# A squeeze-and-excite gate on one core: larger resident slots, reads and stores cut into pieces at the turn between its two passes

## The chip, the cores and the metric

The kernel runs on one core of a Trainium2 chip. The metric is device time in microseconds (us). Every time below is the median of fast runs. Executions of one kernel agree within about 0.2%, so differences of half a microsecond can be told apart when the kernels ran on the same chip in turn. "Span" is the length of the one execution that was profiled; it is about 1.9 us shorter than the timed run.

In the profile, PE is the matmul engine (TensorE) and PEld its weight loads, DVE is VectorE, ACT is ScalarE, POOL is GpSimd and SP is SyncE; a q after the name is that engine's DMA queue. SBUF is the on-chip memory for data, PSUM the one that matmuls write to. "DMA share" is the mean busy share of the core's 16 DMA engines (in short stretches it can read a little over 1), and PEclk is the granted clock of PE as a share of full speed.

## The reference

```python
# x: (1, 256, 256, 384) bf16; w_down: (384, 24); w_up: (24, 384)
def reference(x, w_down, w_up):
    s = x.mean(axis=(1, 2))
    s = _sigmoid(_silu(s @ w_down) @ w_up)
    return x * s[:, None, None, :]
```

The gate needs the mean over the whole input before the first output element can be made. The input is 50.33 MB and does not fit into SBUF. So the kernel makes two passes: it reads everything once for the mean, keeps what it can, and reads the rest a second time.

## The kernel before

Each partition holds 512 rows of 384 bf16 elements; one row over 128 partitions is 128 x 768 = 98,304 B. The rows are cut into 32 chunks of 16. There are 16 slots of one chunk each. In the read phase, PE sums every row with a matmul against ones. The last 16 chunks stay resident. In the second phase VectorE multiplies a chunk in its slot, the ACT queue stores it, and the SP queue reads a missing chunk into a slot whose store has landed.

```python
            def _(sp):                                       # SP queue
                sp.dma_start(wd_sb[:, :, :], ...).then_inc(sem_w, 16)      # weights first
                sp.dma_start(wu_sb[0:RED, :], w_up[:, :]).then_inc(sem_w, 16)
                for t in range(NCH):                         # read phase: 32 chunks of 16 rows
                    ...
                    if t >= S:
                        sp.wait_ge(sem_pe, t - S + 1)
                    sp.dma_start(slots[s][:, 0:nr, :], xr[:, rs:rs + nr, :]).then_inc(sem_rd[s], 16)
                for i, (c, s, is_stream) in enumerate(items):  # second reads
                    ...
                    sp.wait_ge(sem_wr[s], 16 * item_wr_before[i])
                    sp.dma_start(slots[s][:, 0:nr, :], ...).then_inc(sem_rd[s], 16)
            ...
            def _(act):
                ...
                act.wait_ge(sem_pe, NCH)
                for k in range(NK):                          # mean: three copies out of PSUM
                    act.activation(mean3[32 * k:32 * k + 1, 0:P], ps_S[0:1, k * P:(k + 1) * P], ACTF.Copy, scale=inv_count).then_inc(sem_mean3, 1)
                ...
                for i, (c, s, is_stream) in enumerate(items):
                    act.wait_ge(sem_dve, i + 1)              # VectorE: one multiply per chunk
                    act.dma_start(outr[:, rs:rs + nr, :], slots[s][:, 0:nr, :]).then_inc(sem_wr[s], 16)
```

## Time and profile before

| Reading (before) | Value |
|---|---|
| time | 314.41 us (span 312.5) |
| HBM read / written | 75.53 MB / 50.33 MB |
| rate, read phase / second phase | 425 / 430 GB/s |
| first read issued | 1.75 us |
| last read's matmuls start | 123.82 us |
| first multiply starts | 129.64 us |
| first store issued | 133.03 us |

The page of the kernel before, its span in 40 slices (each 7.8 us): busy tenths of each engine, DMA busy tenths and the rate; and the bytes.

```profile
PE   0977787777777777200000000000000000000000
DVE  0000000000000000499999999994444444000000
...
DMA  7999999999999996099999999999999999999998
GB/s 250 431 428 422 425 428 422 425 426 423 425 424 423 425 426 254 0 377 327 429 428 429 429 428 433 433 431 433 429 429 428 429 428 429 429 431 431 433 433 357
...
HBM read 75.53 MB, written 50.33 MB: 403 GB/s over the span
```

The DMA row is full except at the start, the end and one hole at slices 15 and 16 (counted from 0). PE never fills a slice for long and VectorE is idle half of the second phase, so neither sets the pace.

Busy times by stretch, before: start and length in us, busy time (instructions) of each engine, granted PE clock, DMA share, rate.

```profile
core 0: us, PE busy (x) PEld busy (x) DVE busy (x) ACT busy (x) POOL busy (x), PEclk, DMA share, GB/s
8.00:104.00 96.00, 74.36 (x415) 39.22 (x414) 0.00 (x0) 0.00 (x0) 0.00 (x0) 0.98 1.01 425
160.00:260.00 100.00, 0.00 (x0) 0.00 (x0) 72.31 (x23) 0.00 (x0) 0.00 (x0) 0.50 1.01 430
122.00:133.60 11.60, 4.42 (x27) 2.11 (x25) 4.40 (x4) 1.45 (x5) 0.00 (x0) 0.87 0.02 8
```

The first two stretches are at the pace of the DMA engines. In the third, 11.6 us long, the DMA share is 0.02: it stands still. What it waits for is in the timeline of the kernel before (start us, length us, engine, line, instruction, and in brackets the idle time before it).

```profile
0.73 0.42 SPq L136 DMA_DIRECT2D se_wd<-in_w_down_dram  x1
1.21 0.48 SPq L137 DMA_DIRECT2D se_wu<-in_w_up_dram  x1
1.75 11.70 SPq L143 DMA_DIRECT2D se_slot<-in_x_dram  x12
...
123.82 2.77 PE L193 MATMUL se_psS<-se_slot,se_ones 128*32 128x384 bf16 x16 [0.90 <-DMA se_slot<-in_x_dram]
126.63 0.84 ACT L227 ACTIVATE se_mean<-se_psS 1x128 bf16<-1x128 f32 x3 [124.40 <-PE se_psS L193]
...
129.12 0.49 ACT L236 ACTIVATE se_sbc<-se_psu 128x384 bf16<-128x384 f32 x1 [0.74 <-PE se_psu L218]
129.64 6.63 DVE L175 TENSOR_TENSOR se_slot<-se_slot,se_sbc 128x6144 bf16<-128x6144 bf16 x2 [0.95 <-ACT se_sbc L236]
133.03 0.38 ACTq L240 DMA_DIRECT2D out_dram<-se_slot  x1
```

After the last read has landed, PE still has the whole last chunk to sum (2.77 us), ACT copies the mean (0.84), a chain of small steps makes the gate, and VectorE multiplies a whole chunk (3.35 us each) before the first store can be issued.

### The profile page before, as it was taken

The numbers are of one execution on the slowest core, as the hardware profiler recorded it, in microseconds if no ns is written. First come the engines' busy times: TensorE is split into PE (matmuls) and PEld (weight loads), VectorE is DVE, ScalarE is ACT, GpSimd is POOL, SyncE is SP. The second block draws the span as 40 slices with busy tenths as digits, with TensorE's granted clock in tenths as the row PEclk, the third lists the DMA queues.
The fourth block names the chain that finished last, engine by engine and source line by source line (L and its number), as shares of the span: only waits on it lengthen the run. The fifth ranks groups of instructions, "written<-read, shape, count | busy, mean of one in ns | idle before, by whom it ended". The sixth has DMA issues, their size and how long they took to land.

```text
span 312.5 us, 1205 instructions
## 1 busy us (share of the span) xinstructions
PE 92.3 (30%) x517; PEld 48.5 (16%) x517; DVE 106.2 (34%) x40; ACT 2.9 (1%) x7; POOL 0.2 (0%) x4
## 2 busy tenths in 40 slices
PE   0977787777777777200000000000000000000000
PEld 0444344444333444100000000000000000000000
DVE  0000000000000000499999999994444444000000
ACT  1000000000000000100000000000000000000000
POOL 0000000000000000000000000000000000000000
PEclk9999799999999999855555555555555555555555
DMA  7999999999999996099999999999999999999998
GB/s 250 431 428 422 425 428 422 425 426 423 425 424 423 425 426 254 0 377 327 429 428 429 429 428 433 433 431 433 429 429 428 429 428 429 429 431 431 433 433 357
DMA packets 11960, 125.94 MB, mean 403 GB/s; under 512 B 1692, under 2 KB 1716, under 8 KB 1716
## 3 DMA queue, kind: packets, MB, share of 16 engines
q1 hardware_dynamic: 7348, 75.54, 57.7%
q10 hardware_dynamic: 4608, 50.33, 38.1%
q8 instruction: 4, 0.07, 0.1%
HBM read 75.53 MB, written 50.33 MB: 403 GB/s over the span
## 4 chain that ended last, share of the span: by engine, by line
DMA 56%; DVE 14%; another core or an unknown queue 9%; PE 2%; SPq 2%; ACT 0%; issue 0%
DMA se_slot<-in_x_dram 40%; DMA out_dram<-se_slot 16%; DVE se_slot L175 14%; PE se_psS L193 2%; SPq L143 1%; SPq L149 0%; ACT se_mean L227 0%; ACT se_sbc L236 0%; SPq L137 0%; SPq L136 0%; PE se_psu L218 0%; DVE se_dT L165 0%; PE se_psd L209 0%; PE se_psmT L204 0%
## 5 line engine op out<-in xcount | busy, mean ns | idle before, releaser
L175 DVE TENSOR_TENSOR se_slot<-se_slot,se_sbc 128x6144 bf16<-128x6144 bf16 x32 | 105.4, 3353 | 28.6 <-DMA se_slot<-in_x_dram 27.7
L193 PE MATMUL se_psS<-se_slot,se_ones 128*32 128x384 bf16 x512 | 91.5, 334 | 35.1 <-DMA se_slot<-in_x_dram 35.1
L193 PEld LDWEIGHTS se_psS<-se_slot,se_ones 128*32 128x32 bf16 x512 | 48.2, 99 | 78.0 <-DMA se_slot<-in_x_dram 38.4
L162 DVE CAST se_meanT<-se_psmT 128x3 bf16<-128x3 f32 x1 | 0.2, 164 | 126.4 <-PE se_psmT L204 126.4
L227 ACT ACTIVATE se_mean<-se_psS 1x128 bf16<-1x128 f32 x3 | 0.8, 265 | 124.4 <-PE se_psS L193 124.4
L223 ACT ACT_TABLE_LOAD x1 | 1.3, 1283 | 0.7 <-PEq L255 0.7
L218 PE MATMUL se_psu<-se_wu,se_dT 24*128 24x384 bf16 x1 | 0.3, 332 | 0.6 <-DVE se_dT L165 0.6
L236 ACT ACTIVATE se_sbc<-se_psu 128x384 bf16<-128x384 f32 x1 | 0.5, 490 | 0.7 <-PE se_psu L218 0.7
L204 PE MATMUL se_psmT<-se_sel,se_mean 65*128 65x3 bf16 x1 | 0.2, 178 | 0.9 <-ACT se_mean L227 0.9
L165 DVE TENSOR_TENSOR se_dT<-se_psd,se_sig 24x128 bf16<-24x128 f32 x1 | 0.3, 279 | 0.5 <-ACT se_sig L234 0.5
L155 DVE MEMSET se_ones<- 128x32 bf16 x1 | 0.1, 85 | 0.8 <-PEq L255 0.8
L204 PEld LDWEIGHTS se_psmT<-se_sel,se_mean 65*128 65x128 bf16 x1 | 0.1, 96 | 1.3 <-ACT se_mean L227 1.3
L209 PE MATMUL se_psd<-se_meanT,se_wd 128*24 128x1 bf16 x3 | 0.2, 167 | 0.3 <-DVE se_meanT L162 0.3
L160 DVE MEMSET se_sel<- 1x1 bf16 x3 | 0.2, 59 | 0.2
L223 ACT ACTIVATE se_warm<-se_ones 1x8 bf16<-1x8 bf16 x1 | 0.2, 208 | 0.0
L218 PEld LDWEIGHTS se_psu<-se_wu,se_dT 24*128 24x128 bf16 x1 | 0.1, 91 | 0.7 <-DVE se_dT L165 0.7
L209 PEld LDWEIGHTS se_psd<-se_meanT,se_wd 128*24 128x24 bf16 x3 | 0.1, 90 | 0.3 <-DVE se_meanT L162 0.3
L234 ACT ACTIVATE se_sig<-se_psd 24x1 f32<-24x1 f32 x1 | 0.2, 160 | 0.8 <-PE se_psd L209 0.8
L156 DVE MEMSET se_mean<- 128x64 uint32 x1 | 0.1, 112 | 0.0
L255 POOL MEMSET const-bfloat16-1.0<- 128x1 bf16 x1 | 0.1, 101 | 0.0
L255 POOL MEMSET const-uint8-127<- 128x1 uint8 x1 | 0.1, 101 | 0.0
L255 POOL MEMSET const-float32-0.0<- 128x1 f32 x1 | 0.1, 98 | 0.2 <-issue 0.2
(2 smaller groups left out, 0.2 us busy)
## 6 DMA issues: line engine op xcount, KB each, us to landing
se_slot<-in_x_dram SPq DMA_DIRECT2D x48, 1536.0 KB, 31.5
out_dram<-se_slot ACTq DMA_DIRECT2D x32, 1536.0 KB, 43.7
se_wd<-in_w_down_dram SPq DMA_DIRECT2D x1, 18.0 KB
se_wu<-in_w_up_dram SPq DMA_DIRECT2D x1, 18.0 KB
```

The source lines that it names most:

```text
L143: sp.dma_start(slots[s][:, 0:nr, :], xr[:, rs:rs + nr, :]).then_inc(sem_rd[s], 16)
L160: v.memset(sel[32 * k:32 * k + 1, k:k + 1], 1.0).then_inc(sem_init, 1)
L165: v.tensor_tensor(dT[0:RED, 0:P], ps_d[0:RED, 0:1].broadcast_to([RED, P]), sig[0:RED, 0:1].broadcast_to([RED, P]), ALU.mult,).then_inc(sem ...
L175: v.tensor_tensor(slots[s][:, 0:nr, :], slots[s][:, 0:nr, :], s_bc[:, None, :].broadcast_to([P, nr, C]), ALU.mult,).then_inc(sem_dve, 1)
L193: ins = pe.matmul(ps_S[0:M1, 0:C], ones[:, 0:M1], slots[s][:, r, :], start=(mm_i == 0), stop=(mm_i == n_mm - 1),)
L204: pe.matmul(ps_mT[:, 0:NK], mean3[0:32 * (NK - 1) + 1, 0:P], sel[0:32 * (NK - 1) + 1, 0:NK]).then_inc(sem_mT, 1)
L209: ins = pe.matmul(ps_d[0:RED, 0:1], wd_sb[:, k, 0:RED], meanT[:, k:k + 1], start=(k == 0), stop=(k == NK - 1),)
L218: pe.matmul(ps_u[:, 0:C], dT[0:RED, 0:P], wu_sb[0:RED, 0:C]).then_inc(sem_u, 1)
L223: act.activation(warm[0:1, 0:8], ones[0:1, 0:8], ACTF.Sigmoid)
L227: act.activation(mean3[32 * k:32 * k + 1, 0:P], ps_S[0:1, k * P:(k + 1) * P], ACTF.Copy, scale=inv_count,).then_inc(sem_mean3, 1)
L236: act.activation(s_bc[:, 0:C], ps_u[:, 0:C], ACTF.Sigmoid).then_inc(sem_sbc, 1)
L255: nc = _bacc.Bacc("TRN2", target_bir_lowering=False, num_devices=1)
```

## The change

The change keeps the two passes and their order. It makes the slots larger and fewer (14 of 21 rows, 294 rows resident instead of 256, with a smaller reserve for dynamic DMA to make room), cuts the last reads and the first stores into pieces, takes the mean with one VectorE instruction, and moves the weight loads from the head of the SP queue to the ACT queue, late in the read phase. The new GpSimd path and the scratch slot are off with the default arguments.

```diff
-        R = max(1, min(RPP, (16 * 1024) // (C * 2)))
+        R = max(1, min(RPP, 21))                       # chunks: 8 rows, then 24 of 21
...
-        S_fit = max(1, (avail - 1024) // (slot_bytes + 64))
+        S_fit = max(1, (avail - 64) // slot_bytes)     # 14 slots
...
+        piece_plan = _phase1_read_pieces(chunks)
+        # last four chunks: [4,17] [9,12] [6,8,7] [3,5,4,3,2,2,2] rows
...
+            elif s == 0:
+                pieces = make_pieces(nr, list(first_item_pieces))      # 2, 4, 4, 5, 6
+            elif s == 1 or (s == 2 and 1 in pool_slot_set):
+                pieces = make_pieces(nr, [6, 7, 8])
+            elif s == 2:
+                pieces = make_pieces(nr, [10, 11])
+            else:
+                pieces = [(0, nr)]
...
             def _(sp):
-                sp.dma_start(wd_sb[:, :, :], ...)
-                sp.dma_start(wu_sb[0:RED, :], ...)
...
             def _(v):
+                v.wait_ge(sem_pe, NCH)
+                v.tensor_scalar(out=meanr[0:1, 0:C], in0=ps_S[0:1, 0:C], scalar1=inv_count, ...)
...
             def _(act):
-                for k in range(NK):
-                    act.activation(mean3[...], ps_S[...], ACTF.Copy, scale=inv_count)
+                act.wait_ge(sem_pe, max(0, NCH - 3))
+                act.dma_start(wd_sb[:, :, :], ...)
+                act.dma_start(wu_sb[0:RED, :], ...)
...
-    nc = _bacc.Bacc("TRN2", target_bir_lowering=False, num_devices=1)
+    nc = _bacc.Bacc("TRN2", target_bir_lowering=False, num_devices=1, dynamic_dma_scratch_size=256)
```

More of the change, by code (lines that the diff above doesn't have):

```diff
@@ L1, with _phase1_read_pieces @@
 import contextlib
-import math
 import concourse.bass as bass
 from concourse import mybir
+def _phase1_read_pieces(chunks, pe_rate_frac=0.24, min_piece=2, extra=2):
+    pieces_per_chunk = {}
+    rem = 0
+    plan = []
+    for t in reversed(range(len(chunks))):
+        nr = chunks[t][1]
+        cuts_rev = []
+        left = nr
+        while left > 0:
+            cap = max(min_piece, int(pe_rate_frac * rem) + extra)
+            sz = min(left, cap)
+            cuts_rev.append(sz)
+            rem += sz
+            left -= sz
+        sizes = list(reversed(cuts_rev))
+        lo = 0
+        pl = []
+        for sz in sizes:
+            pl.append((lo, lo + sz))
+            lo += sz
+        pieces_per_chunk[t] = pl
+        if len(pl) == 1 and sizes[0] == nr and rem - nr >= 4 * nr:
+            break
+    for t in range(len(chunks)):
+        if t in pieces_per_chunk:
+            plan.append(pieces_per_chunk[t])
+        else:
+            plan.append([(0, chunks[t][1])])
+    return plan
 def bass_standalone__se_block__vision_kernel(
@@ L16, in bass_standalone__se_block__vision_kernel @@
     max_slots=None,
+    use_scratch=False,
+    first_item_pieces=(2, 4, 4, 5, 6),
+    pool_slots=(),
+    pool_piece_rows=7,
 ):
@@ L37, in bass_standalone__se_block__vision_kernel @@
     if rows_per_chunk is None:
-        R = max(1, min(RPP, (16 * 1024) // (C * 2)))
-        while R > 1 and RPP % R != 0:
-            R -= 1
+        R = max(1, min(RPP, 21))
     else:
-        R = int(rows_per_chunk)
+        R = max(1, min(int(rows_per_chunk), RPP))
     chunks = []
+    rem0 = RPP % R
     rs = 0
+    if rem0:
+        chunks.append((0, rem0))
+        rs = rem0
     while rs < RPP:
-        nr = min(R, RPP - rs)
-        chunks.append((rs, nr))
-        rs += nr
+        chunks.append((rs, R))
+        rs += R
     NCH = len(chunks)
@@ L60, in bass_standalone__se_block__vision_kernel @@
         s_bc = E(nc.sbuf_tensor("se_sbc", [P, C], bf16))
-        mean3 = E(nc.sbuf_tensor("se_mean3", [P, P], bf16))
-        sel = E(nc.sbuf_tensor("se_sel", [P, NK], bf16))
+        meanr = E(nc.sbuf_tensor("se_meanr", [P, C], bf16))
         meanT = E(nc.sbuf_tensor("se_meanT", [P, NK], bf16))
@@ L67, in bass_standalone__se_block__vision_kernel @@
         dT = E(nc.sbuf_tensor("se_dT", [P, P], bf16))
-        warm = E(nc.sbuf_tensor("se_warm", [P, 8], bf16))
         ps_S = E(nc.psum_tensor("se_psS", [P, C], f32))
-        ps_mT = E(nc.psum_tensor("se_psmT", [P, NK], f32))
+        ps_mT = E(nc.psum_tensor("se_psmT", [P, NK * 512], f32))
         ps_d = E(nc.psum_tensor("se_psd", [P, 1], f32))
@@ L76, in bass_standalone__se_block__vision_kernel @@
         avail = nc.sbuf_bytes_remaining
-        S_fit = max(1, (avail - 1024) // (slot_bytes + 64))
-        S = min(NCH, S_fit)
+        S_fit = max(1, (avail - 64) // slot_bytes)
+        slots = []
+        if use_scratch and nc.dynamic_dma_scratch_size is not None and nc.dynamic_dma_scratch_size >= slot_bytes:
+            slots.append(nc.alloc_sbuf_tensor_at("se_slot_scr", [P, R, C], bf16, offset=0))
+        S = S_fit + len(slots)
+        S = min(NCH, S)
         if max_slots is not None:
@@ L81, in bass_standalone__se_block__vision_kernel @@
         assert S >= 2 or NCH == 1
-        slots = [E(nc.sbuf_tensor(f"se_slot{i}", [P, R, C], bf16)) for i in range(S)]
+        while len(slots) < S:
+            slots.append(E(nc.sbuf_tensor(f"se_slot{len(slots)}", [P, R, C], bf16)))
+        slots = slots[:S]
         sem_rd = [E(nc.semaphore(f"se_rd{i}")) for i in range(S)]
@@ L89, in bass_standalone__se_block__vision_kernel @@
         sem_ones = E(nc.semaphore("se_onesm"))
-        sem_z = E(nc.semaphore("se_z"))
-        sem_init = E(nc.semaphore("se_init"))
-        sem_mean3 = E(nc.semaphore("se_m3"))
+        sem_mean = E(nc.semaphore("se_mean"))
         sem_mT = E(nc.semaphore("se_mT"))
@@ L99, in bass_standalone__se_block__vision_kernel @@
         sem_sbc = E(nc.semaphore("se_sbcs"))
+        sem_pool = E(nc.semaphore("se_pool"))
         slot_of_chunk = [t % S for t in range(NCH)]
@@ L103, in bass_standalone__se_block__vision_kernel @@
         resident_chunk_of_slot = [max(t for t in range(NCH) if t % S == s) for s in range(S)]
-        items = []
-        for s in range(S):
-            items.append((resident_chunk_of_slot[s], s, False))
-        for b in range(NB):
-            items.append((b, b % S, True))
-        assert len(items) == NCH
-        assert sorted(c for c, _, _ in items) == list(range(NCH))
         fill_cnt = [0] * S
-        wr_cnt = [0] * S
         phase1_fill_idx = []
@@ L118, in bass_standalone__se_block__vision_kernel @@
             phase1_fill_idx.append(fill_cnt[s])
-        item_fill_idx = []
-        item_wr_before = []
-        fill_cnt2 = list(fill_cnt)
-        for (c, s, is_stream) in items:
-            if is_stream:
-                item_wr_before.append(wr_cnt[s])
-                fill_cnt2[s] += 1
-                item_fill_idx.append(fill_cnt2[s])
-            else:
-                item_wr_before.append(None)
-                item_fill_idx.append(phase1_fill_idx[c])
-            wr_cnt[s] += 1
+        piece_plan = _phase1_read_pieces(chunks)
@@ new lines, in bass_standalone__se_block__vision_kernel @@
+        p1_pieces = []
+        extra_piece_sems = 0
+        for t in range(NCH):
+            s = slot_of_chunk[t]
+            pl = []
+            for i, (lo, hi) in enumerate(piece_plan[t]):
+                if i == 0:
+                    pl.append((lo, hi, sem_rd[s], 16 * phase1_fill_idx[t]))
+                else:
+                    sm = E(nc.semaphore(f"se_p1x{extra_piece_sems}"))
+                    extra_piece_sems += 1
+                    pl.append((lo, hi, sm, 16))
+            p1_pieces.append(pl)
@@ new lines, in bass_standalone__se_block__vision_kernel, with make_pieces @@
+        assert extra_piece_sems <= 16
+        def make_pieces(nr, sizes):
+            cuts = [0]
+            for z in sizes:
+                cuts.append(min(nr, cuts[-1] + z))
+            if cuts[-1] < nr:
+                cuts.append(nr)
+            cuts = sorted(set(cuts))
+            return [(cuts[i], cuts[i + 1]) for i in range(len(cuts) - 1)]
+        pool_slot_set = set(int(ps) for ps in pool_slots if 0 <= int(ps) < S)
+        items = []
+        for s in range(S):
+            c = resident_chunk_of_slot[s]
+            nr = chunks[c][1]
+            eng = "pool" if s in pool_slot_set else "dve"
+            if eng == "pool":
+                k = max(1, -(-nr // max(1, int(pool_piece_rows))))
+                base = [nr // k] * k
+                for i in range(nr - sum(base)):
+                    base[i] += 1
+                pieces = make_pieces(nr, base)
+            elif s == 0:
[4 more added lines that the diff above has]
+                pieces = make_pieces(nr, [10, 11])
+            else:
+                pieces = [(0, nr)]
+            items.append(dict(chunk=c, slot=s, stream=False, eng=eng, pieces=pieces, fill_idx=phase1_fill_idx[c]))
@@ new lines, in bass_standalone__se_block__vision_kernel @@
+        wr_cnt = [0] * S
+        fill_cnt2 = list(fill_cnt)
+        for it in items:
+            it["wr_before"] = None
+            wr_cnt[it["slot"]] += len(it["pieces"])
+        for b in range(NB):
+            s = b % S
+            it = dict(chunk=b, slot=s, stream=True, eng="dve", pieces=[(0, chunks[b][1])])
+            it["wr_before"] = wr_cnt[s]
+            fill_cnt2[s] += 1
+            it["fill_idx"] = fill_cnt2[s]
+            wr_cnt[s] += len(it["pieces"])
+            items.append(it)
@@ L131, in bass_standalone__se_block__vision_kernel @@
         total_wr = list(wr_cnt)
+        assert sorted(it["chunk"] for it in items) == list(range(NCH))
         with nc.Block() as block:
@@ L135, in _ @@
             def _(sp):
-                sp.dma_start(wd_sb[:, :, :], w_down.rearrange("(k p) r -> p k r", p=P)).then_inc(sem_w, 16)
-                sp.dma_start(wu_sb[0:RED, :], w_up[:, :]).then_inc(sem_w, 16)
                 for t in range(NCH):
                     s = slot_of_chunk[t]
-                    rs, nr = chunks[t]
+                    rs_, nr = chunks[t]
                     if t >= S:
                         sp.wait_ge(sem_pe, t - S + 1)
-                    sp.dma_start(slots[s][:, 0:nr, :], xr[:, rs:rs + nr, :]).then_inc(sem_rd[s], 16)
-                for i, (c, s, is_stream) in enumerate(items):
-                    if not is_stream:
-                        continue
-                    rs, nr = chunks[c]
-                    sp.wait_ge(sem_wr[s], 16 * item_wr_before[i])
-                    sp.dma_start(slots[s][:, 0:nr, :], xr[:, rs:rs + nr, :]).then_inc(sem_rd[s], 16)
+                    for (lo, hi, sm, _wv) in p1_pieces[t]:
+                        sp.dma_start(slots[s][:, lo:hi, :], xr[:, rs_ + lo:rs_ + hi, :]).then_inc(sm, 16)
+                n_pp = 0
+                for it in items:
+                    if it["eng"] != "pool":
+                        continue
+                    c, s = it["chunk"], it["slot"]
+                    rs_ = chunks[c][0]
+                    for (lo, hi) in it["pieces"]:
+                        n_pp += 1
+                        sp.wait_ge(sem_pool, n_pp)
+                        sp.dma_start(outr[:, rs_ + lo:rs_ + hi, :], slots[s][:, lo:hi, :]).then_inc(sem_wr[s], 16)
+                for it in items:
+                    if not it["stream"]:
+                        continue
+                    c, s = it["chunk"], it["slot"]
+                    rs_, nr = chunks[c]
+                    sp.wait_ge(sem_wr[s], 16 * it["wr_before"])
+                    sp.dma_start(slots[s][:, 0:nr, :], xr[:, rs_:rs_ + nr, :]).then_inc(sem_rd[s], 16)
                 for s in range(S):
@@ L155, in _ @@
                 v.memset(ones[:, :], 1.0).then_inc(sem_ones, 1)
-                v.memset(mean3[:, :], 0.0).then_inc(sem_z, 1)
-                v.memset(sel[:, :], 0.0).then_inc(sem_z, 1)
-                v.wait_ge(sem_z, 2)
-                for k in range(NK):
-                    v.memset(sel[32 * k:32 * k + 1, k:k + 1], 1.0).then_inc(sem_init, 1)
+                v.wait_ge(sem_pe, NCH)
+                v.tensor_scalar(
+                    out=meanr[0:1, 0:C],
+                    in0=ps_S[0:1, 0:C],
+                    scalar1=inv_count,
+                    scalar2=None,
+                    op0=ALU.mult,
+                ).then_inc(sem_mean, 1)
                 v.wait_ge(sem_mT, 1)
-                v.tensor_copy(meanT[:, 0:NK], ps_mT[:, 0:NK]).then_inc(sem_meanT, 1)
+                v.tensor_copy(meanT[:, 0:NK], ps_mT[:, 0:NK * 512:512]).then_inc(sem_meanT, 1)
                 v.wait_ge(sem_sig, 1)
@@ L171, in _ @@
                 v.wait_ge(sem_sbc, 1)
-                for i, (c, s, is_stream) in enumerate(items):
-                    rs, nr = chunks[c]
-                    v.wait_ge(sem_rd[s], 16 * item_fill_idx[i])
-                    v.tensor_tensor(
-                        slots[s][:, 0:nr, :],
-                        slots[s][:, 0:nr, :],
-                        s_bc[:, None, :].broadcast_to([P, nr, C]),
-                        ALU.mult,
-                    ).then_inc(sem_dve, 1)
+                for it in items:
+                    if it["eng"] != "dve":
+                        continue
+                    s = it["slot"]
+                    first = True
+                    for (lo, hi) in it["pieces"]:
+                        if first:
+                            v.wait_ge(sem_rd[s], 16 * it["fill_idx"])
+                            first = False
+                        v.tensor_tensor(
+                            slots[s][:, lo:hi, :],
+                            slots[s][:, lo:hi, :],
+                            s_bc[:, None, :].broadcast_to([P, hi - lo, C]),
+                            ALU.mult,
+                        ).then_inc(sem_dve, 1)
+            @block.gpsimd
+            def _(g):
+                pool_items = [it for it in items if it["eng"] == "pool"]
+                if pool_items:
+                    g.wait_ge(sem_sbc, 1)
+                for it in pool_items:
+                    s = it["slot"]
+                    first = True
+                    for (lo, hi) in it["pieces"]:
+                        if first:
+                            g.wait_ge(sem_rd[s], 16 * it["fill_idx"])
+                            first = False
+                        g.tensor_tensor(
+                            slots[s][:, lo:hi, :],
+                            slots[s][:, lo:hi, :],
+                            s_bc[:, None, :].broadcast_to([P, hi - lo, C]),
+                            ALU.mult,
+                        ).then_inc(sem_pool, 1)
             @block.tensor
@@ L184, in _, with row_mms @@
                 pe.wait_ge(sem_ones, 1)
-                n_mm = sum(nr for _, nr in chunks)
-                mm_i = 0
-                for t in range(NCH):
-                    s = slot_of_chunk[t]
-                    rs, nr = chunks[t]
-                    pe.wait_ge(sem_rd[s], 16 * phase1_fill_idx[t])
-                    ins = None
-                    for r in range(nr):
-                        ins = pe.matmul(
+                n_mm_total = sum(nr for _, nr in chunks)
+                mm_i = [0]
+                def row_mms(s, lo, hi):
+                    ins_ = None
+                    for r in range(lo, hi):
+                        ins_ = pe.matmul(
                             ps_S[0:M1, 0:C],
@@ L196, in _ @@
                             slots[s][:, r, :],
-                            start=(mm_i == 0),
-                            stop=(mm_i == n_mm - 1),
-                        )
-                        mm_i += 1
-                    ins.then_inc(sem_pe, 1)
-                pe.wait_ge(sem_mean3, NK)
-                pe.wait_ge(sem_init, NK)
-                pe.matmul(ps_mT[:, 0:NK], mean3[0:32 * (NK - 1) + 1, 0:P], sel[0:32 * (NK - 1) + 1, 0:NK]).then_inc(sem_mT, 1)
+                            start=(mm_i[0] == 0),
+                            stop=(mm_i[0] == n_mm_total - 1),
+                        )
+                        mm_i[0] += 1
+                    return ins_
+                for t in range(NCH):
+                    s = slot_of_chunk[t]
+                    ins = None
+                    for (lo, hi, sm, wv) in p1_pieces[t]:
+                        pe.wait_ge(sm, wv)
+                        ins = row_mms(s, lo, hi)
+                    ins.then_inc(sem_pe, 1)
+                pe.wait_ge(sem_mean, 1)
+                ins = None
+                for k in range(NK):
+                    ins = pe.matmul(
+                        ps_mT[:, k * 512:k * 512 + 1],
+                        meanr[0:1, k * P:(k + 1) * P],
+                        ones[0:1, 0:1],
+                        start=True,
+                        stop=True,
+                    )
+                ins.then_inc(sem_mT, 1)
                 pe.wait_ge(sem_meanT, 1)
@@ L222, in _ @@
                 act.wait_ge(sem_ones, 1)
-                act.activation(warm[0:1, 0:8], ones[0:1, 0:8], ACTF.Sigmoid)
-                act.wait_ge(sem_pe, NCH)
-                act.wait_ge(sem_z, 2)
-                for k in range(NK):
-                    act.activation(
-                        mean3[32 * k:32 * k + 1, 0:P],
-                        ps_S[0:1, k * P:(k + 1) * P],
-                        ACTF.Copy,
-                        scale=inv_count,
-                    ).then_inc(sem_mean3, 1)
+                act.activation(sig[32:33, 0:1], ones[32:33, 0:1], ACTF.Sigmoid)
+                act.wait_ge(sem_pe, max(0, NCH - 3))
+                act.dma_start(wd_sb[:, :, :], w_down.rearrange("(k p) r -> p k r", p=P)).then_inc(sem_w, 16)
+                act.dma_start(wu_sb[0:RED, :], w_up[:, :]).then_inc(sem_w, 16)
                 act.wait_ge(sem_d, 1)
@@ L236, in _ @@
                 act.activation(s_bc[:, 0:C], ps_u[:, 0:C], ACTF.Sigmoid).then_inc(sem_sbc, 1)
-                for i, (c, s, is_stream) in enumerate(items):
-                    rs, nr = chunks[c]
-                    act.wait_ge(sem_dve, i + 1)
-                    act.dma_start(outr[:, rs:rs + nr, :], slots[s][:, 0:nr, :]).then_inc(sem_wr[s], 16)
+                n_piece = 0
+                for it in items:
+                    if it["eng"] != "dve":
+                        continue
+                    c, s = it["chunk"], it["slot"]
+                    rs_ = chunks[c][0]
+                    for (lo, hi) in it["pieces"]:
+                        n_piece += 1
+                        act.wait_ge(sem_dve, n_piece)
+                        act.dma_start(outr[:, rs_ + lo:rs_ + hi, :], slots[s][:, lo:hi, :]).then_inc(sem_wr[s], 16)
     return nc
```

## The prediction

> **What bounds the kernel now.** The bytes on the DMA engines. The page's 40 slices show the DMA at 9 tenths everywhere but at the start, at slices 15 to 17 and at the end, at 422 to 433 GB/s. The Trainium skill ("DMA: Bandwidth & Descriptors", section "Where 436 GB/s comes from") puts the ceiling at 435.2 GB/s; this trace runs at 424 while only reading (stretch 60 to 110 us) and 430 while reading and writing (150 to 250 us), 97% to 99% of it. What is left to gain: fewer bytes, less DMA standstill. HBM read is 75.53 MB (the 50.33 MB input, and 16 of 32 chunks read a second time), written 50.33 MB. By stretches, the DMA moves nothing from about 122.3 to 133.6 us: about 11.3 us between the read phase and the first write. The chain of waits in this gap: last semaphore at 123.8 (1.5 us after the data stopped), 2.79 us of 16 matmuls, 0.85 us for three ACT copies of the mean, 2.1 us for the small chain to the gate, 3.35 us for the first VectorE multiply of 16 rows, then issue and first byte.
>
> **What the change does.**
> 1. Slots: 14 of 21 rows (294 rows resident) replace 16 of 16 rows (256). 11 second reads, 218 rows instead of 256. 38 rows x 98,304 B = 3.74 MB less; at 430 GB/s, -8.7 us. All critical, since DMA is saturated from 150 us to the end.
> 2. First store: the first multiply covers 2 rows instead of 16. At 3,352 ns per 16 rows, an estimated 0.45 us instead of 3.35: -2.9 us. VectorE makes a row in 0.21 us, DMA takes 0.229 us per row, so the small pieces keep the DMA fed.
> 3. Last reads cut into pieces down to 2 rows: PE (0.174 us a row) follows the DMA (0.232 us a row) and has some 2 to 3 rows left at the end: an estimated 0.5 us instead of 2.8: -2.3 us.
> 4. Mean: one VectorE scaling of 1x384 instead of three ACT copies, but three tiny matmuls instead of one: an estimated -0.3 us.
> 5. Weight loads leave the head of the sync queue, where their issues took 0.42 and 0.48 us: the first read is issued at about 0.7 instead of 1.75 us: -1.0 us.
> 6. Costs: the last read pieces and first store pieces use packets of 1.5 to 4.6 KB in place of 12 KB, and more semaphore updates: +0.5 us, an estimate.
>
> Sum: -8.7 -2.9 -2.3 -0.3 -1.0 +0.5 = -14.7 us. Nearly all is on the critical path.
>
> **Predicted: 299.7 us, range 296.5 to 303.0 (8 in 10). Chances: faster by over 2% 0.96, within 2% 0.03, slower 0.01.**
>
> **What would show it.** HBM read 71.8 MB. The DMA gap about 6 us instead of 11.3. PE matmuls after the last read's semaphore under 1 us. First store issued under 1 us after the gate is written. First read issued near 0.7 us. Mixed rate still about 430 GB/s.
>
> **What would make it wrong.** The rate of the DMA: 1% is 3 us. Packets of 16,128 B start at other addresses than those of 12,288 B, and could run slower or faster. Between 139 and 149 us the rate fell to 209 to 455 GB/s while the first second-reads joined the stores, about 2 us lost; with larger slots this dip may grow or vanish. If the weight loads late in the read phase delay the last pieces, point 5 comes back.

## The result, and the profile after

The changed kernel takes 300.03 us (8 runs, 299.88 to 300.24) against 314.41 us (12 runs). The ratio is 0.9541, 95% interval 0.9532 to 0.9551. Ratios here are the mean time of one kernel's fast runs over that of the other's of the same rounds, so not quite the ratio of the medians.

The page of the changed kernel: slices of 7.5 us, and bytes.

```profile
DVE  0000000000000000199999999999943550000000
...
DMA  8999999999999999289999999999999999999997
GB/s 300 430 430 430 424 435 422 430 430 422 432 426 428 416 419 389 98 332 391 384 415 447 417 443 422 439 426 430 435 424 441 419 445 417 447 417 443 422 439 324
...
HBM read 71.80 MB, written 50.33 MB: 409 GB/s over the span
```

The hole in the DMA row has shrunk, and 3.73 MB fewer are read. By stretches, in the columns shown before:

```profile
8.00:104.00 96.00, 72.91 (x407) 39.38 (x408) 0.00 (x0) 0.00 (x0) 0.00 (x0) 0.98 1.01 428
160.00:260.00 100.00, 0.00 (x0) 0.00 (x0) 71.33 (x18) 0.00 (x0) 0.00 (x0) 0.50 1.01 431
122.00:128.00 6.00, 2.35 (x15) 0.72 (x13) 2.62 (x6) 0.65 (x2) 0.00 (x0) 0.91 0.04 15
```

The standstill is 6 us instead of 11.6. The edges of these stretches are set by eye; by events, from the last read's landing to the first store's issue, 9.21 us (123.82 to 133.03) became 3.89 us (123.07 to 126.96). The rates have hardly moved. The skill's ceiling of 435.2 GB/s, which the prediction leans on, still stands above both averages (single slices read up to 447). That figure is for the ports of SBUF; the same section says that for transfers between HBM and SBUF a lower limit of about 358 GB/s on the HBM side binds, and both kernels, each on one core, run well above it: here the measurement decides. The timeline of the changed kernel, the same events:

```profile
0.73 9.03 SPq L219 DMA_DIRECT2D se_slot<-in_x_dram  x11
...
122.59 0.11 PEld L306 LDWEIGHTS se_psS<-se_slot,se_ones 128*32 128x32 bf16 x2 [0.36 <-DMA se_slot<-in_x_dram]
123.07 0.11 PEld L306 LDWEIGHTS se_psS<-se_slot,se_ones 128*32 128x32 bf16 x2 [0.37 <-DMA se_slot<-in_x_dram]
123.61 0.55 DVE L244 TENSOR_SCALAR se_meanr<-se_psS 1x384 bf16<-1x384 f32 x1 [122.72 <-PE se_psS L306]
...
125.85 0.49 ACT L359 ACTIVATE se_sbc<-se_psu 128x384 bf16<-128x384 f32 x1 [0.73 <-PE se_psu L347]
126.37 9.04 DVE L271 TENSOR_TENSOR se_slot<-se_slot,se_sbc 128x768 bf16<-128x768 bf16 x8 [0.95 <-ACT se_sbc L359]
126.96 7.19 ACTq L369 DMA_DIRECT2D out_dram<-se_slot  x7
```

The last two-row piece lets PE go on at 123.07 us, and 0.5 us later the sum is finished. The first store is issued 0.6 us after the first multiply starts. But the last piece lands only 0.75 us earlier than the last chunk did before (123.82), although the first read was issued 1.02 us earlier and the rate was a little higher: something in the read phase was given back. The experiments look for it.

### The profile page after: what moved, and what is told of

Same layout as the page of the kernel before. It is cut to its first block, busy times and chain, and to the rows that moved or that the text cites. A ratio compares the mean times of both kernels' runs of the same rounds, so it can differ in the third digit from the quotient of the medians.

```text
span 298.4 us, 1197 instructions
## 1 busy us (share of the span) xinstructions
PE 93.8 (31%) x519; PEld 49.3 (17%) x519; DVE 106.0 (36%) x36; ACT 2.1 (1%) x4; POOL 0.2 (0%) x4
## 3 DMA queue, kind: packets, MB, share of 16 engines
HBM read 71.80 MB, written 50.33 MB: 409 GB/s over the span
## 4 chain that ended last, share of the span: by engine, by line
DMA 45%; DVE 16%; SPq 8%; PE 8%; another core or an unknown queue 5%; issue 0%; ACT 0%
DMA se_slot<-in_x_dram 29%; DVE se_slot L271 16%; DMA out_dram<-se_slot 16%; SPq L219 8%; PE se_psS L306 7%; DVE se_meanr L244 0%; ACT se_sbc L359 0%; PE se_psu L347 0%; SPq L236 0%; DVE se_dT L255 0%; PE se_psd L338 0%; PE se_psmT L326 0%; DVE se_meanT L252 0%; ACT se_sig L357 0%
## 5 line engine op out<-in xcount | busy, mean ns | idle before, releaser
L271 DVE TENSOR_TENSOR se_slot<-se_slot,se_sbc 128x8064 bf16<-128x8064 bf16 (+8 forms) x32 | 105.0, 3348 | 15.2 <-DMA se_slot<-in_x_dram 14.2
L306 PE MATMUL se_psS<-se_slot,se_ones 128*32 128x384 bf16 x512 | 93.0, 339 | 30.6 <-DMA se_slot<-in_x_dram 30.6
L306 PEld LDWEIGHTS se_psS<-se_slot,se_ones 128*32 128x32 bf16 x512 | 48.9, 100 | 74.3 <-DMA se_slot<-in_x_dram 36.3
```

Of the source, the lines that this page charges most:

```text
L271: v.tensor_tensor(slots[s][:, lo:hi, :], slots[s][:, lo:hi, :], s_bc[:, None, :].broadcast_to([P, hi - lo, C]), ALU.mult,).then_inc(sem_dv ...
L306: ins_ = pe.matmul(ps_S[0:M1, 0:C], ones[:, 0:M1], slots[s][:, r, :], start=(mm_i[0] == 0), stop=(mm_i[0] == n_mm_total - 1),)
```

## The experiments

There were eleven runs. All gave correct results. "Against the changed kernel" means against its 300.03 us, or 299.88 us; the kernel before was between 314.49 and 314.56 us.

### 1. The slots: bytes or chunk size

Theory: the slots gain only by the bytes that are not read again. Rivals: the chunk size changes the rate; or stores set the second phase and bytes do not count. Three edits, each alone in the changed kernel:

```diff
# a_r16_s16                       # a_r16_s18                      # a_s13
-    rows_per_chunk=None,         -    rows_per_chunk=None,        -    max_slots=None,
-    max_slots=None,              -    max_slots=None,             +    max_slots=13,
+    rows_per_chunk=16,           +    rows_per_chunk=16,
+    max_slots=16,                +    max_slots=18,
```

> Changed kernel with 16 slots of 16 rows as before (256 rows resident), all else kept. Theory (bytes): HBM read returns to 75.5 MB, 38 rows x 98,304 B / 430 GB/s = 8.7 us longer, so 308.7 us. Rival (chunk size itself matters: in the read phase the trace shows 428 GB/s with 21-row chunks and 424 with 16): another 1 us, 309.5 to 310 us, with 424 in the read phase. Rival 2 (stores, not bytes, set the second phase): under 3 us longer.

> Changed kernel with 18 slots of 16 rows (288 rows resident). Theory (bytes): 6 rows more than the changed kernel, +1.4 us, 301.4 us, and 7.3 us less than the run with 16 slots. Rival (chunk size matters for the rate): +2.5 us or more.

> Changed kernel with 13 slots instead of 14, nothing else: 21 rows, 2.06 MB, are read again. Theory (bytes at 430 GB/s): +4.8 us, 304.8 us. Rival (part of the gain of the slots came from the chunk size, which is the same here, or fewer slots also starve the stores): clearly less than 4.5 or more than 5.2 us.

| Run | rows resident | us | against the changed kernel | bytes alone, at 430 GB/s |
|---|---|---|---|---|
| a_r16_s16 | 256 | 309.02 | +9.0 | +8.7 |
| a_r16_s18 | 288 | 302.04 | +2.0 | +1.4 |
| a_s13 | 273 | 304.69 | +4.8 | +4.8 |

With 16-row chunks the kernel also makes its cuts anew (the last four chunks are read in 13 pieces, not 14); that is part of what these two edits change.

With the chunk size kept (a_s13) the bytes alone give the time exactly. Between the two runs with 16-row chunks, 32 rows are worth 6.98 us, where bytes alone give 7.3. With the chunk size changed as well, 0.3 to 0.6 us are left over. In the read phase (8 to 104 us) these runs moved 426 GB/s and the changed kernel 428; that half per cent of about 118 us is an estimated 0.55 us. So the theory holds, and the rival of the chunk size is right about half a microsecond, not more. The rival of the stores falls.

The same slots alone in the kernel before:

```diff
-        R = max(1, min(RPP, (16 * 1024) // (C * 2)))
-        while R > 1 and RPP % R != 0:
-            R -= 1
+        R = 21
...
+    chunks = [(0, RPP % R)] + [(RPP % R + R * i, R) for i in range(RPP // R)]
...
+        S_fit = 14
...
+    nc = _bacc.Bacc("TRN2", ..., dynamic_dma_scratch_size=256)
```

> Kernel before with the new slots alone (14 of 21 rows, 294 resident, 8-row first chunk). Theory (bytes, with the chunk's tail on PE and on VectorE in full): -8.7 us for 38 rows, but the last chunk leaves PE 21 rows (+0.85 us) and the first multiply covers 21 rows (+1.0 us): 307.6 us. Rival (the slots are worth the full 9.0 us that undoing them cost): 305.4 us.

It took 306.49 us, 8.06 less than the kernel before (314.55). That is 1.1 us better than my expectation and 1.1 us worse than the rival's. The expected losses are in its trace: PE works 3.60 us after the last semaphore, not 2.79, and the first store is issued at 134.49 us, not 133.03. From the first store to the end it needs 170.2 us (304.7 - 134.49) where the kernel before needs 179.5; the bytes account for 8.7 of these 9.3 us. The last semaphore also came 0.36 us earlier. So large chunks alone cost some 1.5 us at the turn, which is what the pieces are for, and gain about 1 us elsewhere that I had not booked.

### 2. The first stores whole

```diff
-                pieces = make_pieces(nr, list(first_item_pieces))
+                pieces = make_pieces(nr, [nr])
...
-                pieces = make_pieces(nr, [6, 7, 8])
+                pieces = make_pieces(nr, [nr])
...
-                pieces = make_pieces(nr, [10, 11])
+                pieces = make_pieces(nr, [nr])
```

> Changed kernel with the first three resident slots multiplied and stored whole (21 rows) instead of in pieces. The first multiply takes 4.34 us instead of 0.56. Theory (the standstill before the first store counts in full): first store 3.8 us later, less about 0.6 us that the small first stores lose in rate: 303.1 to 303.8 us. Rival (head start partly given back, since the first second read waits for the whole first slot anyway and VectorE paces the first stores): at most +2 us.

It took 302.89 us: +2.9 us, a little under the range of the theory and well over that of the rival. The timeline of this run:

```profile
126.16 17.16 DVE L271 TENSOR_TENSOR se_slot<-se_slot,se_sbc 128x8064 bf16<-128x8064 bf16 x4 [0.95 <-ACT se_sbc L359]
130.55 8.88 ACTq L369 DMA_DIRECT2D out_dram<-se_slot  x3
```

The first store was issued 4.39 us after the first multiply started (130.55 - 126.16) instead of 0.59 (126.96 - 126.37), so the head start is 3.8 us. From the first store to the end it needed 170.55 us (301.1 - 130.55) and the changed kernel 171.44 (298.4 - 126.96). So 0.9 us of the head start is given back with ten small stores in place of three. It is not all a price of their number. In the first 2 us after the first store's issue the changed kernel moved 155 GB/s at a DMA share of 0.42, this run 258 GB/s at 0.61: an estimated 0.5 us, and the lower share fits a DMA that has no further piece to store yet. In the next 6 us both were fully busy, but the changed kernel moved 404 GB/s and this run 430: an estimated 0.4 us.

### 3. The last reads whole

```diff
-        piece_plan = _phase1_read_pieces(chunks)
+        piece_plan = [[(0, nr_)] for _, nr_ in chunks]
```

> Changed kernel with all reads of the first phase whole. PE has 21 rows (3.6 us) left after the last semaphore instead of 2 (0.5 us): +3.1 us. Theory: the cost of the small pieces returns, about 1.1 us by the rate of 376 to 418 GB/s between 100 and 122 us, so net +2.0 us, 302.0 us, and the rate from 100 us on is 428 again. Rival (the low rate there is due to the weight loads issued at 110.6 us, not to the pieces): net +3.1 us, and the rate stays low around 112 us.

It took 302.08 us: +2.05 us, as the theory said. The timeline of this run shows both parts:

```profile
121.92 3.59 PE L306 MATMUL se_psS<-se_slot,se_ones 128*32 128x384 bf16 x21 [1.34 <-DMA se_slot<-in_x_dram]
125.55 0.55 DVE L244 TENSOR_SCALAR se_meanr<-se_psS 1x384 bf16<-1x384 f32 x1 [124.66 <-PE se_psS L306]
```

The last read is there at 121.92 us instead of 123.07, so the pieces cost 1.15 us of reading; PE then needs 3.6 us instead of 0.5. By stretches, the changed kernel first and then this run:

```profile
104.00:114.00 10.00, 8.85 (x54) 4.88 (x52) 0.00 (x0) 0.00 (x0) 0.00 (x0) 1.00 1.01 417
114.00:120.00 6.00, 4.94 (x30) 2.40 (x28) 0.00 (x0) 0.00 (x0) 0.00 (x0) 1.00 1.04 378
```

```profile
104.00:114.00 10.00, 7.55 (x46) 4.15 (x45) 0.00 (x0) 0.00 (x0) 0.00 (x0) 1.00 0.99 423
114.00:120.00 6.00, 4.70 (x30) 2.61 (x29) 0.00 (x0) 0.00 (x0) 0.00 (x0) 1.00 0.99 400
```

The DMA engines are as busy with the pieces but move less: 378 GB/s against 400 (and the whole reads end in this stretch, which lowers their 400). The weight loads are in both runs at the same place, so they are not the cause of the 1.15 us. But the rate of this one stretch is no measure of the pieces alone: with the pieces kept and the weight loads moved to the head of the ACT queue (a_w_act below) it was 399 GB/s, although the last piece then landed only 0.11 us earlier. Ten more DMAs for the reads cost 1.15 us: an estimated 0.12 us for each DMA more. Whether it is the number of DMAs or the smaller pieces (1.5 to 13 KB a partition instead of 16 KB) was not separated.

### 4. The weight loads

```diff
# a_w_sp                                       # a_w_act
             def _(sp):                                     def _(act):
+                sp.dma_start(wd_sb[...], ...)  +                act.dma_start(wd_sb[...], ...)
+                sp.dma_start(wu_sb[...], ...)  +                act.dma_start(wu_sb[...], ...)
...                                            ...
             def _(act):                       -                act.wait_ge(sem_pe, max(0, NCH - 3))
-                act.wait_ge(sem_pe, ...)      -                act.dma_start(wd_sb[...], ...)   # late
-                act.dma_start(...)  # both    -                act.dma_start(wu_sb[...], ...)
```

> Changed kernel with the two weight loads back at the head of the sync queue. Theory of the prediction (issue time at the head counts in full): first read issued at about 1.7 instead of 0.7 us, +1.0 us, 301.0 us. Rival (the loads' small packets cost DMA time wherever they run, and late in the saturated read phase they cost what they saved at the head): 300.0 to 300.3 us.

> Changed kernel with the two weight loads at the head of the scalar queue, with no wait: they take no issue time from the sync queue and run while the DMA engines are still filling. If late small packets cost anything (rival of the run beside it): 299.2 to 299.7 us. If only the issue time counts: 300.0 us, no change, or slower if the first read is delayed by the small packets.

At the head of the SP queue: 300.78 us, +0.75. At the head of the ACT queue: 299.95 us, no change. The last piece landed at 123.98 us in the first run and at 122.96 us in the second, against 123.07 us. The issue time at the head of the queue is what counts, not the loads themselves. In the timeline of the run with the loads at the head of the SP queue, the first read again has to wait for them:

```profile
0.73 0.42 SPq L213 DMA_DIRECT2D se_wd<-in_w_down_dram  x1
1.20 0.48 SPq L214 DMA_DIRECT2D se_wu<-in_w_up_dram  x1
1.73 1.29 SPq L221 DMA_DIRECT2D se_slot<-in_x_dram  x3
```

The Trainium skill says so in "DMA: Bandwidth & Descriptors", section "Issuing engines are not separate DMA queues": starting DMAs on several engines "will only save the time on the sequencer it takes to initiate the DMA". This case agrees: two issues of 0.42 and 0.48 us, and 0.75 us of the whole time.

### 5. A version with fewer bytes: 18 rows in PSUM

If bytes are what counts, any memory that holds rows across the turn should pay. Seven PSUM banks hold 18 rows. The Trainium skill ("PSUM — Partial Sum Buffer", "The four PSUM rules") says that DMA cannot touch PSUM (no run here tries it), so VectorE copies rows there in the read phase, in which it is otherwise idle, and later multiplies them from PSUM into a slot. The edit, shortened:

```diff
+    chunks.append((0, 18))                     # first chunk; then 11 rows, then 23 of 21
...
-        ps_S / ps_mT / ps_d / ps_u             # six banks
+        ps_A = E(nc.psum_tensor("se_psA", [P, 512], f32))     # one bank for all small results
+        ps_st = E(nc.psum_tensor("se_stash", [P, 7 * 512], f32))
...
                     if t >= S:
                         sp.wait_ge(sem_pe, t - S + 1)
+                    if t == S:
+                        sp.wait_ge(sem_st, 7)
...
+                v.wait_ge(sem_rd[0], 16)
+                for i in range(7):             # bf16 pairs copied as f32 words
+                    v.tensor_copy(ps_st[:, lo_:hi_], x0[:, lo_:hi_]).then_inc(sem_st, 1)
...
+                    if it.get("stash"):        # after the resident items
+                        v.wait_ge(sem_wr[s], 16 * it["wr_before"])
+                        v.tensor_tensor(slots[s][:, 0:ST, :], <ps_st as bf16 rows>, s_bc[...], ALU.mult)
```

> The changed kernel once more, as the base for the two beside it on the same chip: 300.0 us, within 0.2 us.

> Changed kernel that keeps 18 more rows in PSUM: VectorE, idle in the read phase, copies the first 18 rows from their slot to seven PSUM banks, and in the second phase multiplies them from there into slot 0 once that is stored; all small results share the remaining bank. 18 rows, 1.77 MB, are not read again. Theory (bytes at 430 GB/s, VectorE has 15 us of idle time in the second phase): -4.1 us, 295.9 us. Rival (second reads are hidden behind the backlog of stores, so their number no longer matters at this point): under 1 us.

The changed kernel again took 299.88 us, this version 296.46 us: ratios to the kernel before of 0.9535 and 0.943. That is 3.4 us better, not 4.1, but far from the rival's "under 1 us". The page of this run, and its group for the multiply out of PSUM:

```profile
HBM read 70.03 MB, written 50.33 MB: 408 GB/s over the span
```

```profile
L280 DVE TENSOR_TENSOR se_slot<-se_stash,se_sbc x1: 3762/3762/3762, 186.5 to 186.5; 128x6912 bf16<-128x6912 bf16 x1
```

Since the first second read now came later (138.85 us), and the stretch of 134 to 150 us ran at 372 GB/s instead of 386, I supposed that the missing 0.7 us lay there, and gave slot 0 back to the second reads:

```diff
-            s = b % S
+            s = b - 1 if b > 0 else NB - 1
```

> The kernel with 18 rows in PSUM, with slot 0 given to the first second read and the rows from PSUM multiplied into slot 10 instead. In the run before, the first second read was issued at 138.85 us instead of 133.89, and the stretch of 134 to 150 us ran at 372 GB/s instead of 386. If that dip is what the 18 rows lost against the estimate of -4.1 us (they gave -3.4): 0.5 us better, 295.9 us. Rival (the dip comes whenever second reads join and only shifts): 296.4 us.

It took 296.69 us: no gain. The dip did fill (404 GB/s from 134 to 150 us, first second read at 133.88), but the time did not follow. In this version VectorE waited 39 us for slot 10 before its multiply out of PSUM, and from 292.0 to 293.5 us, near the end of the span of 295.0 us, the DMA share was only 0.3; that would fit some DMA engines finishing late, but it was not tested. So that supposition fell, and where the 0.7 us went stays open. The first PSUM version is the fastest kernel here.

## Why the prediction was right

The prediction was 299.7 us, the measured time 300.03. The change is worth 14.4 us against 14.7 predicted. Every sign it named came in: 71.80 MB read, a standstill of 6 us, PE finishing 0.5 us after the last piece, a first store 0.6 us after the first multiply starts, a first read issued at 0.73 us, 431 GB/s in the second phase. Three profiles, one execution each, give a ledger that adds up by itself (us in the trace; the middle one is the changed kernel with the old slots):

| Event | before | old slots (a_r16_s16) | changed |
|---|---|---|---|
| first read issued | 1.75 | 0.73 | 0.73 |
| first multiply starts | 129.64 | 126.93 | 126.37 |
| first store issued | 133.03 | 127.52 | 126.96 |
| end of the span | 312.5 | 307.3 | 298.4 |
| first store to end | 179.5 | 179.8 | 171.4 |

All that does not touch the slots moves the first store 5.5 us forward and lengthens what follows by 0.3. The slots shorten what follows by 8.3 us and the read phase by 0.6.

Point by point:

1. **Slots, -8.7.** Right: undoing them cost 9.0 us, and 21 rows fewer cost 4.8 us, as the bytes say.
2. **First store, -2.9.** Right in size before costs. The first multiply took 0.56 us, not the estimated 0.45. I had divided the 3,352 ns by rows and forgotten the fixed part: 4,342 ns for 21 rows and 558 ns for 2 give 199 ns a row and 160 ns fixed. The Trainium skill has that term ("VectorE: DVE Perf Modes", section "The TRN2 errata — SBUF-src ops pay a fixed extra latency per instruction": a measured fixed term of about 150 cycles), and this trace agrees with it: at the 0.96 GHz that the skill's opening page ("Trainium Kernel Development and Optimization", section "NeuronCore Architecture") gives for this engine, 150 cycles are an estimated 156 ns.
3. **PE's tail, -2.3.** Right: 0.5 us for 2.79.
4. **Mean, -0.3.** From the end of the sum to the end of the copy of the mean vector, 1.27 us (126.63 to 127.90) became 1.02 us (123.61 to 124.63). This was read from the traces, not tested by itself.
5. **Weight loads, -1.0.** Nearly: +0.75 us when put back.
6. **Costs, +0.5.** This is the term that was mis-sized. The pieces cost 1.15 us in the reads and 0.9 us in the stores, about 2 us; and about half of the 0.9 was lost while the DMA was not full, which the prediction's smaller packets and semaphore updates do not cover. It went unseen in the sum because of gains that nobody had booked; one is that larger chunks were read at 428 instead of 425 or 426 GB/s. The terms measured one at a time (first store 3.35 - 0.56 and PE's tail 2.79 - 0.5, both before costs) sum to 9.0 + 2.8 + 2.3 + 0.25 + 0.75 - 2.05 = 13.05 us, 1.3 less than the 14.4 measured. So the mechanism was right, but that the total came within 0.3 us is partly luck. Where the 1.3 us lie is not shown. What a piece costs may depend on what surrounds it: with the old slots and also ten small stores, the time from the first store to the end was only 0.3 us longer than before.

The dip where second reads join the stores, which the prediction feared, stayed: 374 GB/s from 134 to 150 us before, 385 in the changed kernel.

## What to carry to other kernels

When the DMA is saturated, write the time as bytes over the measured rate plus the time in which the DMA stands still; here that gave the value of a row of residency (0.229 us) well enough to predict three experiments on the slots to within 0.7 us (the fourth, b_slots, missed by 1.1). A standstill between two phases is shortened by making the last input and the first output small, but cutting has a price (here about 0.12 us for each read more; for the stores it was 0.9 us in one kernel and 0.3 us in another), so cut only those next to the gap. Look for idle memory and idle engines before tuning further: 18 rows in PSUM, carried by an idle VectorE, were worth more than the pieces at either side of the turn.

## What the Trainium skill lacked or had wrong

- "VectorE: DVE Perf Modes", section "The perf-mode tier table", gives 1x for a two-tensor operation with any PSUM operand. Here the bf16 multiply with one operand in PSUM took 3,762 ns (one instruction; 3,757 in the second PSUM version) for 6,912 elements a partition (0.544 ns each), against 4,342 ns for 8,064 from SBUF (0.538 ns each): no slower. The page's section "Why PSUM operands drop a tier" (a cap at 2x for PSUM operands) fits the run; the table does not.
- "DMA: Bandwidth & Descriptors" gives 512 B as the smallest transfer for full rate. For a DMA by itself it also has a fixed cost (about 2 us, measured on the path from GpSimd), but it has no price for one more DMA on a queue that is already full. Here ten more DMAs for the same bytes, in pieces of 1.5 KB a partition and up, cost 1.15 us of reading (last read at 123.07 instead of 121.92 us).
- "SBUF — State Buffer", section "SBUF size: 192, 224, or 256?", takes 16 KiB off for DMA descriptors and does not say that a kernel can have them back. A kernel that issues no DMA from GpSimd ran correctly with that reserve set to 256 B and 14 slots of 16,128 B, that is 225,792 B a partition; the 38 rows gained by this and by tighter slots were worth 8.7 to 9.0 us.
